# One 32-byte tile moved to the far end of SBUF, so that every tile starts at a multiple of 128 bytes

## The chip, the core and the metric

The kernel runs on one core of a Trainium2 chip. Its time is device microseconds of one execution. Five engines work side by side: TensorE (PE in the profile, its weight loads PEld), VectorE (DVE), ScalarE (ACT), GpSimd (POOL) and SyncE (SP), which issues the DMAs here. On-chip memory (SBUF) has 128 partitions; a tile of shape [128, n] has one row of n elements in each of them, and all rows of a tile begin at the same byte address.

## What is computed

All arrays are float32 (batch 8, heads 8, sequence 576, head size 64; 4608 tokens, model width 512):

```python
kv = einsum('bhsd,bhse->bhde', k, v)           # linear attention
out = einsum('bhsd,bhde->bhse', q, kv)
x = out / sqrt(mean(out * out, -1) + 1e-6) * g_norm
h = x @ w_in                                    # 512 -> 2048
x = (s * relu(h) ** 2 + b) @ w_out              # 2048 -> 512
h = maximum(maximum(x @ w1, x @ w2), x @ w3)    # 512 -> 768
return h @ w_out2                               # 768 -> 512
```

## The kernel before

TensorE multiplies in fp32r, a four-byte format of less precision, so each operand is split into a high and a low part (`hilo`: ScalarE copies the high part, VectorE subtracts) and each product is three matmuls: high by high, high by low, low by high. A matmul loads 128 columns of a weight tile (512 bytes of each row) and streams up to 512 columns of the other operand past it (2048 bytes of each row), which is called the moving operand below.

Tokens go in nine tiles of 512. In the first stage, per token tile and per chunk f of 16 chunks of the 2048 wide layer, `u1` (line 326) makes 12 matmuls `h<-xh,w` and `h<-xl,w`, `u1_end` squares and splits, and two chunks later `u2` (line 349) makes 12 matmuls `y<-gh,w` and `y<-gl,w`. Attention for the next tiles is put between them (`s1`, `s3`, `s4`: lines 215, 244, 284, 285; `ones` is the weight tile of lines 284 and 285). Until all weights are split (the first 300 us) `w_float` and `w_parts` turn them from 64 to 32 bits on ScalarE and VectorE. In the second stage `v1` (line 488) forms the products of the next layer by a seven-product scheme from prepared weight tiles `wc`, and `v2_steps` (line 557) the last product. The weights of the second stage are prepared in the last two token tiles of the first stage and pass through DRAM (`combine`, `pair_load`).

A scheduling layer sets each engine's order when the program is built. SBUF addresses come from pools that are stacked from the left end or, with `side="right"`, from the right end:

```python
const = pool("const", 1)                              # left, first
wpa = pool("wpa", 2 * FA, st=low, side="right")       # weights f < 8
wpb = pool("wpb", 2 * (KF - FA), st=mlp1)             # left: weights f >= 8
t = (wpa if f < FA else wpb).tile([P, 2, DM], F32R, tag="w", name=nm)   # FA = 8
cst = const.tile([P, 8], F32, name="cst")             # 32 bytes in a row
w2p["a"] = pool("w2a", 2, side="right")               # wc of q % 3 == 0, 1
w2p["b"] = pool("w2b", 1)                             # left: wc of q % 3 == 2
```

`ones` is the first tile, at byte 1152 (a multiple of 128). `cst` (scales, biases and two constants as single columns) follows it and takes 32 bytes, and every size after it is a multiple of 128, so that all later tiles of the left side begin 32 bytes past a multiple of 128. Those of the right side (`wpa`, `w2a` and the high parts of the tokens in the second stage, pool `ta`) begin 96 bytes past one. The moving operands of the first stage (`xh`, `xl`, `gh`, `gl`) lie left; those of the second stage lie right where they are high parts and left where they are low parts (with the first super-tile, which has 256 columns in place of 512, both lie right).

Of the kernel before, what the change touches and what calls it, by code (L numbers as in the profile page):

```python
# [8 lines left out]
F32 = mybir.dt.float32  # L9
# [11 lines left out]
P = 128  # L21
# [3 lines left out]
def fused_kernel(ctx, tc, qt, kv, kvr, g_norm, w_in, w_out, s, b, w1, w2, w3, w_out2, out):  # L25
# [22 lines left out]
    def pool(name, bufs, space=None, st=ctx, side="left"):  # L48
        kw = {"space": space} if space is not None else {"side": side, "reuse_waits": "tile"}
        return st.enter_context(tc.tile_pool(name=name, bufs=bufs, **kw))  # L50


    mlp1, attn, low = (ctx.enter_context(ExitStack()) for _ in range(3))
    const = pool("const", 1)
    dram = pool("dram", 1, DRAM)
    wpa = pool("wpa", 2 * FA, st=low, side="right")
    rawp = pool("rawp", 2, st=mlp1)
# [16 lines left out]
    EARLY = 2  # L74
    start = [wpb.tile([P, NP + 2, P], F32, tag="w", name=f"start{i}") for i in range(EARLY)]
    onesf, zero = start[0][:, NP, :], start[0][:, NP + 1, :]
    cst = const.tile([P, 8], F32, name="cst")
    g_sb, sb_sb, lnb, exb = cst[:, 0:1], cst[:, 1:3], cst[:, 3:4], cst[:, 4:5]
    kvbd = [const.tile([P, 2, P], F32R, name=f"kvbd{p}") for p in range(NP)]
    y_dr = [dram.tile([P, KD, TW], F32, name=f"y_dr{t}") for t in range(NTILE)]  # L80
# [742 lines left out]
```

## Time and profile before

| | us |
|---|---|
| median of 3 runs | 1486.7 (1486.1 to 1487.91) |
| the profiled execution's own time | 1486.8 |
| its span, first to last instruction | 1485.0 |
| PE busy | 1442.6 |
| VectorE busy | 901.0 |
| ScalarE busy | 618.8 |

The profiled execution agrees with the median to 0.1 us, so its span and the 1.8 us around it are the base of all sums. A busy PE says little by itself, since matmuls overlap in its records: one of 512 columns is recorded with some 390 ns while the next starts 230 ns after it. How quickly they follow each other is seen in the chain of work that ended last, which counts matmuls in a row and the time from the first to the end of the piece.

### The profile page before, as it was taken

The numbers are of one execution on the slowest core, as the hardware profiler recorded it, in microseconds if no ns is written. First come the engines' busy times: TensorE is split into PE (matmuls) and PEld (weight loads), VectorE is DVE, ScalarE is ACT, GpSimd is POOL, SyncE is SP. The second block draws the span as 40 slices with busy tenths as digits, with TensorE's granted clock in tenths as the row PEclk, the third lists the DMA queues.
The fourth block names the chain that finished last, engine by engine and source line by source line (L and its number), as shares of the span: only waits on it lengthen the run. The fifth ranks groups of instructions, "written<-read, shape, count | busy, mean of one in ns | idle before, by whom it ended". The sixth has DMA issues, their size and how long they took to land.

```text
span 1485.0 us, 18915 instructions
## 1 busy us (share of the span) xinstructions
PE 1442.6 (97%) x7010; PEld 1175.6 (79%) x7010; DVE 901.0 (61%) x1722; ACT 618.8 (42%) x1255; POOL 11.7 (1%) x41
## 2 busy tenths in 40 slices
PE   6799999999999999999999999989999999999998
PEld 4678877788888888888888888977888888888887
DVE  6899989874445454454545556647573672673561
ACT  5665457444455445455544443223231241232221
POOL 0000000000000000000000000000000000000000
PEclk9999999999999999999999999999999999999999
DMA  6556565731111112111013689976553553551521
GB/s 206 160 184 193 176 205 188 226 119 40 40 46 47 53 32 68 47 46 43 15 47 135 232 314 307 387 260 220 198 192 121 198 180 136 194 198 68 188 100 57
DMA packets 66556, 217.77 MB, mean 147 GB/s; under 512 B 7968, under 2 KB 19232, under 8 KB 60704
## 3 DMA queue, kind: packets, MB, share of 16 engines
q1 hardware_dynamic: 66464, 216.56, 42.7%
q8 instruction: 55, 0.90, 0.2%
q14 instruction: 37, 0.30, 0.1%
HBM read 165.41 MB, written 51.12 MB: 146 GB/s over the span
## 4 chain that ended last, share of the span: by engine, by line
PE 85%; DVE 6%; DMA 5%; ACT 3%; issue 1%; SPq 0%; ACTq 0%; DVEq 0%
PE y L349 23%; PE h L326 23%; PE r L488 14%; PE x L488 11%; PE o L557 10%; DMA raw<-in_w_out 1%; DMA raw<-in_w_in 1%; PE ops L244 1%; PE kvps L215 1%; DMA raw<-in_w 1%; DVE tb L108 1%; PE mps L282 1%; DMA wc<-wc_dr 1%; DMA out<-e 1%; ACT ta L105 0%
## 5 line engine op out<-in xcount | busy, mean ns | idle before, releaser
L326 PE MATMUL h<-xh,w 128*128 128x512 f32 (+1 forms) x1176 | 391.9, 394 | 3.4 <-ACT w L90 1.5
L349 PE MATMUL y<-gh,w 128*128 128x512 f32 (+1 forms) x1176 | 387.9, 391 | 2.3 <-ACT gh L337 2.2
L326 PEld LDWEIGHTS h<-xh,w 128*128 128x128 f32 x1176 | 221.5, 190 | 53.3 <-ACT xh L90 2.5
L349 PEld LDWEIGHTS y<-gh,w 128*128 128x128 f32 x1176 | 220.9, 189 | 51.1 <-ACT gh L337 3.6
L326 PE MATMUL h<-xl,w 128*128 128x512 f32 (+1 forms) x588 | 230.2, 392 | 0.1
L349 PE MATMUL y<-gl,w 128*128 128x512 f32 (+1 forms) x588 | 229.0, 390 | 0.0
L336 DVE SCALAR_TENSOR_TENSOR r<-r,cst 128x512 f32<-128x512 f32 (+1 forms) x147 | 108.7, 740 | 130.8 <-ACT r L335 130.1
L338 DVE SCALAR_TENSOR_TENSOR gl<-r,cst,gh 128x512 fp32r<-128x512 f32 (+1 forms) x147 | 108.8, 740 | 123.9 <-ACT gh L337 123.4
L496 ACT ACTIVATE s<-x 128x512 f32<-128x512 f32 (+1 forms) x135 | 74.8, 554 | 247.4 <-PE x L488 241.6
L337 ACT ACTIVATE gh<-r,cst 128x512 fp32r<-128x512 f32 (+1 forms) x147 | 104.9, 714 | 150.1 <-PE y L349 145.5
L335 ACT ACTIVATE r<-h 128x512 f32<-128x512 f32 (+1 forms) x147 | 86.5, 589 | 177.2 <-PE h L326 156.9
L501 DVE TENSOR_TENSOR c<-r,s 128x512 f32<-128x512 f32 (+1 forms) x135 | 81.9, 634 | 91.0 <-ACT s L496 90.6
L557 PE MATMUL o<-wo,hh 128*128 128x512 f32 x432 | 133.2, 390 | 0.3 <-ACT hh L90 0.3
L326 PEld LDWEIGHTS h<-xl,w 128*128 128x128 f32 x588 | 111.8, 190 | 23.5 <-DVE xl L91 0.5
L349 PEld LDWEIGHTS y<-gl,w 128*128 128x128 f32 x588 | 110.7, 188 | 21.7 <-DVE gl L338 0.2
L557 PEld LDWEIGHTS o<-wo,hh 128*128 128x128 f32 x432 | 80.7, 188 | 17.6 <-ACT hh L90 1.0
L557 PE MATMUL o<-wo,hl 128*128 128x512 f32 x216 | 83.8, 389 | 0.0
L501 DVE TENSOR_TENSOR u<-r,s 128x512 f32<-128x512 f32 (+1 forms) x45 | 28.7, 638 | 67.8 <-PE r L488 67.8
L105 ACT ACTIVATE ta<-raw 128x512 f32<-128x512 f32 x56 | 37.7, 674 | 44.6 <-DMA raw<-in_w_out 18.3
L488 PE MATMUL r<-b21h,wc 128*128 128x512 f32 x144 | 51.3, 395 | 4.6 <-ACT b21h L90 4.6
L488 PE MATMUL x<-t2h,wc 128*128 128x512 f32 x144 | 50.8, 393 | 1.1 <-ACT t2h L90 1.1
L488 PE MATMUL x<-t3h,wc 128*128 128x512 f32 x144 | 50.8, 393 | 0.8 <-ACT t3h L90 0.8
(140 smaller groups left out, 2066.8 us busy)
## 6 DMA issues: line engine op xcount, KB each, us to landing
wc<-wc_dr SPq DMA_DIRECT2D x45, 1792.0 KB, 7.4
kv<-in_kv SPq DMA_DIRECT2D x32, 512.0 KB, 4.3
y_dr<-st SPq DMA_DIRECT2D x56, 256.0 KB, 3.3
raw<-in_w_out SPq DMA_DIRECT2D x22, 512.0 KB, 3.7
raw<-in_w SPq DMA_DIRECT2D x18, 512.0 KB, 4.1
out<-e SPq DMA_DIRECT2D x36, 256.0 KB, 2.0
raw<-in_w_in SPq DMA_DIRECT2D x16, 512.0 KB, 3.9
y<-y_dr SPq DMA_DIRECT2D x32, 256.0 KB, 4.8
```

The source lines that it names most:

```text
L105: nc.scalar.activation(out=af, in_=high.bitcast(F32), func=ACTF.Abs)
L108: nc.vector.scalar_tensor_tensor(out=tb, in0=high, scalar=0xC0000000, in1=tb, op0=ALU.bitwise_and, op1=ALU.bitwise_or)
L326: nc.tensor.matmul(h[:, :n], lhsT=w[:, z, kk, :], rhs=x[:, kk, o:o + n], start=(i == 0), stop=(i == 3 * KD - 1))
L335: nc.scalar.activation(out=rn, in_=h[:, :n], func=ACTF.Relu)
L336: nc.vector.scalar_tensor_tensor(out=rn, in0=rn, scalar=sb_sb[:, 0:1], in1=rn, op0=ALU.mult, op1=ALU.mult)
L337: nc.scalar.activation(out=gh[:, :n], in_=rn, func=ACTF.Identity, bias=sb_sb[:, 1:2])
L338: nc.vector.scalar_tensor_tensor(out=gl[:, :n], in0=rn, scalar=sb_sb[:, 1:2], in1=gh[:, :n].bitcast(F32), op0=ALU.add, op1=ALU.subtract)
L349: nc.tensor.matmul(yt[t, o][j][:, :n], lhsT=w[:, z, c], rhs=r[:, :n], start=(f == fa and i == 0), stop=(f == fb - 1 and i == 2))
L488: nc.tensor.matmul(ps, lhsT=w[:, z, POS[c], kk * P:(kk + 1) * P], rhs=x, start=(first and i == 0), stop=(i == 3 * KD // 2 - 1), skip_group ...
L496: nc.scalar.activation(out=t, in_=ps, func=ACTF.Copy)
L501: nc.vector.tensor_tensor(out=o, in0=ps, in1=t, op=ALU.add)
L557: nc.tensor.matmul(acc[b], lhsT=l[:, o:o + P], rhs=wob[m][:, z, :], start=(m == 0 and i == 0), stop=(m == KM - 1 and i == 2))
```

## The change

`cst` leaves the left pool for one of its own, the first from the right end, and is declared with 96 bytes of a row in place of 32. The 32 bytes ahead of the left tiles are gone, and those of the right side move down by 96 bytes.

```diff
     const = pool("const", 1)
+    rim = pool("rim", 1, side="right")
...
-    cst = const.tile([P, 8], F32, name="cst")
+    cst = rim.tile([P, 24], F32, name="cst")
     g_sb, sb_sb, lnb, exb = cst[:, 0:1], cst[:, 1:3], cst[:, 3:4], cst[:, 4:5]
```

In the built programs the instructions of each engine, their order and their waits are the same. What differs is the SBUF address of every tile but `ones`. Counted over all SBUF tiles of the program, 1,975 that began 32 or 96 bytes past a multiple of 128 now begin at one. All of them are now an odd multiple of 128 bytes, not a multiple of 256. Addresses in PSUM and DRAM stay.

## Rows read from the trace of the kernel before

**Rows 1.** The page's part 1: busy time, share of the span, instructions.

```profile
PE 1442.6 (97%) x7010; PEld 1175.6 (79%) x7010; DVE 901.0 (61%) x1722; ACT 618.8 (42%) x1255; POOL 11.7 (1%) x41
```

**Rows 2.** Groups by line and shape: count, busy us, mean ns of one.

```profile
L326 PE MATMUL h<-xh,w 128*128 128x512 f32 x1128 | 379.3, 396 | 1.6 <-ACT xh L90 1.1 <-ACT r L335 0.4
L349 PE MATMUL y<-gh,w 128*128 128x512 f32 x1128 | 375.9, 394 | 0.0
L326 PE MATMUL h<-xl,w 128*128 128x512 f32 x564 | 222.6, 395 | 0.0
...
L557 PE MATMUL o<-wo,hh 128*128 128x512 f32 x432 | 133.2, 390 | 0.3 <-ACT hh L90 0.3
...
L488 PE MATMUL x<-b11h,wc 128*128 128x512 f32 x144 | 51.5, 398 | 0.0
...
L488 PE MATMUL x<-b11l,wc 128*128 128x512 f32 x72 | 28.7, 399 | 0.0
```

**Rows 3.** The chain, 483 to 545 us, one token tile: start us, us, what.

```profile
483.92 2.80 PE h L326 x12
...
489.80 0.44 PE ops L244 x3
490.24 2.80 PE h L326 x12
...
520.99 2.72 PE h L326 x12
...
527.39 2.73 PE h L326 x12
...
533.45 2.75 PE h L326 x12
536.21 0.12 PE mps L284
536.33 0.11 PE mps L285
```

**Rows 4.** The chain, 1118 to 1182 us, second stage.

```profile
1117.87 4.08 PE o L557 x18
...
1137.05 2.75 PE r L488 x12
...
1146.77 2.80 PE r L488 x12
...
1156.47 2.75 PE r L488 x12
...
1175.81 2.80 PE r L488 x12
```

**Rows 5.** The chain, 925 to 960 us, second stage with 256 columns.

```profile
930.93 0.72 PE r L488 x6
...
944.05 9.14 DMA wc<-wc_dr
...
954.25 0.68 PE x L488 x6
```

**Rows 6.** Stretches: length, busy us (count) of PE, PEld, DVE, ACT, POOL, PEclk, DMA.

```profile
0.00:74.00 74.00, 53.13 (x356) 39.17 (x357) 55.47 (x149) 45.44 (x111) 4.91 (x19) 0.95 0.57 183
74.00:297.00 223.00, 215.22 (x1036) 171.34 (x1035) 206.84 (x429) 124.14 (x248) 2.15 (x7) 0.98 0.63 195
297.00:860.00 563.00, 563.00 (x2795) 459.47 (x2794) 286.37 (x552) 270.60 (x577) 4.62 (x15) 1.00 0.22 71
860.00:960.00 100.00, 98.39 (x551) 86.20 (x550) 66.20 (x133) 38.75 (x75) 0.00 (x0) 1.00 0.90 326
960.00:1040.00 80.00, 71.60 (x358) 58.66 (x357) 45.83 (x86) 23.33 (x46) 0.00 (x0) 0.98 0.69 251
1040.00:1485.00 445.00, 441.29 (x1924) 360.74 (x1922) 240.29 (x376) 116.54 (x199) 0.00 (x0) 1.00 0.42 153
```

**Rows 7.** VectorE groups by shape: count, busy us, mean ns of one.

```profile
L501 DVE TENSOR_TENSOR c<-r,s 128x512 f32<-128x512 f32 x108 | 71.3, 687 | 73.2 <-ACT s L496 73.0
...
L501 DVE TENSOR_TENSOR c<-r,s 128x256 f32<-128x256 f32 x27 | 10.6, 421 | 17.8 <-ACT s L496 17.6
```

## The prediction

> **What bounds the kernel now.** I read the page's busy times first. PE is busy for 97% of the span, VectorE for 61% [rows 1]. The stretches say where that holds: from 297 to 860 us PE's busy time is the whole stretch, from 1040 us nearly, at a granted clock of 1.00, which is the level of 2.4 GHz, while VectorE and the DMA engines have room [rows 6]. There the time is the number of matmuls times the distance between their starts. Two stretches are not so. From 74 to 297 us VectorE is busy for 206.84 of 223 us, and from 860 to 1040 us the DMA engines are busy at a share of 0.90 and then 0.69 and PE stands idle for some 10 us [rows 6]; once PE waits 9.14 us for a weight tile `wc` [rows 5].
>
> So the view that decides is the chain, read for the distance from one matmul to the next. It has four different answers for matmuls of the same shape:
> - first stage, weights of the left pool (f from 8 on): 2.72 to 2.75 us for 12, so 226.7 to 229.2 ns each [rows 3]
> - first stage, weights of the right pool (f below 8): 2.80 us for 12, 233.3 ns [rows 3]
> - second stage: 2.75 us for 12 with `wc` at the right (two of three), 229.2 ns, and 2.80 with `wc` at the left (every third), 233.3 ns [rows 4]
> - the last product, all operands at the left: 4.08 us for 18, 226.7 ns [rows 4]
>
> A right operand begins 96 bytes past a multiple of 128, a left one 32. The pattern is: weights and moving operand with the same offset follow each other every 226.7 ns, with different offsets every 233.3 ns. The sides could differ for another reason than the offset, but `ones` lies at the left and has offset 0: with it as the next weights the distance is 0.12 us at 256 columns, with weights of offset 32 next it is 0.11 [rows 3]. The step of 10 ns in which the chain is printed makes this weak, but it points at the offset and not at the side.
>
> The second thing to see is what is left when the offsets agree. 256 columns with equal offsets take 0.72 us for 6, 120.0 ns [rows 5], and 512 take 226.7: 256 more columns cost 106.7 ns, one column per cycle of 2.4 GHz. By that rate 512 columns are 213.3 ns and 256 are 106.7, so both carry a surplus of 13.3 ns; 320 columns, at 0.44 us for 3 [rows 3], carry 146.7 - 133.3 = 13.3 too. And 13.3 ns are 32 columns, 128 bytes of a row. A row of 2048 bytes that starts inside a unit of 128 bytes touches 17 units, not 16; 17 times 13.3 ns is 226.7, and 9 and 11 units give the other two. That reading is an estimate of mine. A fixed price of 32 cycles per matmul would give the same three numbers. Against both in their strict form, 256 columns with unequal offsets take 0.68 us for 6, 113.3 ns [rows 5]: a surplus of half a unit, 64 bytes.
>
> **The change part by part.** No instruction is added, removed or moved.
>
> *Offsets become equal.* All weights and all moving operands now have offset 0. At the least this takes the 233.3 ns rows to 226.7. There are 3384 matmuls of 512 columns on lines 326 and 349 (1128 + 564 each; line 349's `gl` as many as `xl`), 1512 on line 488 (seven products of 144 + 72) and 648 on line 557 (432 and half as many) [rows 2]. The first take (233.3 + 227.9) / 2 = 230.6 ns in the mean, 227.9 being that of 2.72, 2.73 and 2.75 us for 12; the second (2 x 229.2 + 233.3) / 3 = 230.6; the third 226.7. To 226.7 this saves 4896 x 3.9 ns = 19 us.
>
> *Rows begin at a unit.* What the remaining 13.3 ns become is shown by no row, for no moving operand of before has offset 0. Bounds: all of it goes (213.3 ns, nothing below one column per cycle) or none (226.7). Between them lies 220.0, one half unit left, by the 113.3 ns row, where a half unit was left. I hold that the cut unit goes, and do not know whether a half unit stays, so I take the middle of 213.3 and 220.0, a surplus of 3.3 ns. That saves 4896 x 14.0 + 648 x 10.1 ns = 75.0 us, and on some 618 matmuls of 256 and 320 columns (378 of the first super-tile, 240 of attention) about 9 ns each, 5.6 us: 80.6 us. With none left it is 93.4 + 7.5 = 101 us; with a half unit left 56.2 + 3.4 = 60 us.
>
> The Trainium skill has a rule for the warm distance ("TensorE: Matmul & The Clock Gate", Back-to-back issue gap): N / 2.4 GHz plus 2.5 ns, 215.7 ns at 512 columns. By it the saving would be some 86 us before what is given back; no row here comes below 226 ns.
>
> *Given back.* Matmuls become 14 / 230 = 6.1% shorter. Of PE's 53 us before 74 us that is 3.2 us, and I count none: PE waits there for loads and VectorE. From 74 to 297 us it is 13.1 us; VectorE is at 93% and is not made shorter, so I keep a third and give back 8.7. From 860 to 1040 us it is 10.4 us of 170; the DMA engines are nearly full, so I give back half, 5.2. Together 17 us [rows 6].
>
> *VectorE, ScalarE, DMA.* If a cut unit cost VectorE too, it would be at most 64 bytes, 16 elements; an element costs (687 - 421) / 256 = 1.04 ns [rows 7], so 17 ns of an instruction, and for the 578 instructions before 297 us [rows 6] 10 us at most. Its 512-element time is one number in both pools, so I take nothing and keep the 10 us as a bound. Columns of `cst` are read as before, from another address. The transfers' bytes and rows stay; I take nothing for them, hidden by the matmuls except at 860 to 1040 us.
>
> Sum: 80.6 - 17.1 = 63.5 us; 1486.8 - 63.5 = 1423 us. With a half unit left 60 x 0.79 = 47 us and 1440; with none 101 x 0.79 = 80 us and 1407.
>
> **The rivals.**
>
> *Only the mismatch goes.* The 13.3 ns are a price of every fp32r matmul (a weight switch, say), not of a cut unit. For it: the same 13.3 at three widths. Against it: the 113.3 ns row, which undercuts it. 19 us less a fifth: 1472 us (1465 to 1479).
>
> *Nothing changes.* The sides differ by place and not by offset, and the rest is fixed. For it: side and offset go together for all operands but `ones`; against it: the `ones` rows. 1486.8 us. The Trainium skill speaks for this case ("SBUF — State Buffer", Specifications): it gives 16 bytes as the unit in which rows are read, and every offset of before is a multiple of that; in "TensorE: Matmul & The Clock Gate" (Step-by-step) the next weights are loaded through a port of their own and take nothing from the running matmul. The rows of 2.72 and 2.80 us disagree with the second.
>
> *Slower: aligned rows collide.* Both streams now begin a unit at the same byte, so if the two collide once more per matmul when they are in step, each pays a half unit more, 6.7 ns. For it: at 256 columns equal offsets cost 120.0 ns and unequal 113.3 [rows 5]. Against it: at 512 columns it is the other way round. All matmuls of 512 at 233.3 cost 4896 x 2.7 + 648 x 6.6 ns = 17.5 us, the smaller ones 4: 1508 us. It decides once the mean distance at 512 columns is above today's 230.1 ns.
>
> **How the numbers follow.** What a measurement of this kernel can tell from no change is about 0.2%, 3 us. Chances: the forecast, 1407 to 1440 us, 0.60, with 1423 as its time; still less than that (VectorE or the stretch before 297 us gains too) 0.05; only the mismatch 0.20; nothing 0.08; slower 0.07. The range from 1405 to 1475 us takes in the first and the third and leaves out 2 in 10. Faster 0.85, same 0.08, slower 0.07.
>
> **What would show it.** In the chain of the changed kernel one piece of 12 matmuls should take the same time in the first stage for all f and in the second for all q: 2.60 us (216.7 ns), 2.56 with no surplus, 2.64 with a half unit, 2.72 if only the mismatch goes, 2.72 and 2.80 as before if nothing does. VectorE's 687 ns should stay. From 74 to 297 us the same work should end some 4 us earlier, with VectorE's busy share at 95% or more; that would show what is given back. The forecast is wrong if the distance stays at 226 ns or above, or if it falls and the time is kept by waits for VectorE or `wc` that are not there now.

## The result, and the profile after

The changed kernel takes 1472.12 us (median of 4 runs, 1471.08 to 1474.7) beside 1487.31 of the kernel before: a ratio of 0.9898, with a 95% interval from 0.9879 to 0.9917. It is faster by 1.0%. The forecast of 1423 us was wrong, in size and not in direction; 1472 us is the time that the prediction gave to its rival "only the mismatch goes"; it lies at the far end of the whole range and outside the forecast's own, 1407 to 1440.

The page's busy times of the changed kernel, which answer to [rows 1]:

```profile
PE 1428.1 (97%) x7010; PEld 1175.7 (80%) x7010; DVE 900.1 (61%) x1722; ACT 619.1 (42%) x1255; POOL 11.7 (1%) x41
```

The chain of the changed kernel in the same token tile as [rows 3] (start us, us, what; line 326 is now 327, and so on):

```profile
479.03 2.72 PE h L327 x12
...
491.64 2.72 PE h L327 x12
...
515.68 2.72 PE h L327 x12
...
528.14 2.75 PE h L327 x12
530.88 0.12 PE mps L285
531.00 0.12 PE mps L286
...
539.94 2.72 PE h L327 x12
```

The chain in the second stage, three consecutive q, for [rows 4]:

```profile
1116.05 2.72 PE r L489 x12
...
1125.57 2.72 PE r L489 x12
...
1135.09 2.72 PE r L489 x12
```

In the second stage, where there were 2.75 and 2.80 us for 12 matmuls, there is now one number, 2.72, with right weights (the first piece) and left ones (the third), and for every q. In the first stage the 2.80 is gone, and 2.72 is what a piece takes that follows another piece of 12. A piece behind attention takes 2.74 to 2.75 us (2.95 behind `kvps`), as such pieces with left weights did before, so those 2 or 3 hundredths are no matter of offsets. So the difference between the sides is gone. But 2.72 is also the least that was there before: 226.7 ns for 512 columns, with the 13.3 ns over one column per cycle that the forecast took away. The two `mps` pieces of 256 columns were 0.12 and 0.11 us in [rows 3] and are 0.12 and 0.12 now, at equal offsets.

The chain near 940 us, for [rows 5]:

```profile
926.22 11.37 DMA wc<-wc_dr
...
938.67 0.72 PE x L489 x6
...
944.94 0.71 PE x L489 x6
```

With 256 columns equal offsets stay at 118 to 120 ns, as before; the 0.68 us of [rows 5] were those of unequal ones. The 9.14 us of `wc` in [rows 5] and the 11.37 us here are the time of a transfer that the chain follows back, and not a wait of PE, as the prediction read them. PE's own idle time before a `wc` was this in the kernel before (us in total, times, longest), and it is 0.2 us now:

```profile
PE r L488 <- DMA wc<-wc_dr: 1.5, 1, 1.5
```

The stretches, for [rows 6] (length, busy us and count of PE, PEld, DVE, ACT, POOL; granted clock; DMA share and GB/s):

```profile
0.00:74.00 74.00, 53.62 (x361) 39.71 (x362) 57.01 (x153) 46.72 (x114) 4.90 (x19) 0.96 0.58 185
74.00:297.00 223.00, 215.03 (x1043) 173.17 (x1043) 206.64 (x428) 123.63 (x245) 2.24 (x7) 0.98 0.63 198
297.00:860.00 563.00, 563.00 (x2828) 465.44 (x2827) 291.14 (x559) 275.01 (x583) 4.61 (x15) 1.00 0.23 76
860.00:960.00 100.00, 98.31 (x548) 85.37 (x547) 61.22 (x127) 35.09 (x71) 0.00 (x0) 1.00 0.91 329
960.00:1040.00 80.00, 72.56 (x362) 59.99 (x361) 48.85 (x88) 24.35 (x48) 0.00 (x0) 0.98 0.64 228
1040.00:1485.00 445.00, 425.59 (x1878) 352.05 (x1876) 235.28 (x369) 114.28 (x196) 0.00 (x0) 1.00 0.41 149
```

The counts show where the time came from. In the same 563 us PE starts 2828 matmuls and not 2795, 33 more; to 297 us it is 12 more (1404 and not 1392), and from 860 to 1040 us 1 more (910 and not 909). From 1040 us to the end of the span, 1469.3 us, PE has 1878 matmuls left in 429.3 us, where it had 1924 in 445.0: 228.6 ns each and not 231.3. The gain is made where PE has matmuls of 512 columns with unequal offsets one after another. From 860 to 1040 us there is none, and the DMA share of 0.91 need not be the reason: of some 900 matmuls that the kernel before starts there, only 69 are of 512 columns and have unequal offsets. VectorE is no quicker (for [rows 7]):

```profile
L502 DVE TENSOR_TENSOR c<-r,s 128x512 f32<-128x512 f32 x108 | 71.3, 688 | 70.5 <-ACT s L497 69.6
```

### The profile page after: what moved, and what is told of

Read it like the earlier page. It is cut to its first block, busy times and chain, and to the rows that moved or that the text cites. A ratio compares the mean times of both kernels' runs of the same rounds, so it can differ in the third digit from the quotient of the medians.

```text
span 1469.3 us, 18915 instructions
## 1 busy us (share of the span) xinstructions
PE 1428.1 (97%) x7010; PEld 1175.7 (80%) x7010; DVE 900.1 (61%) x1722; ACT 619.1 (42%) x1255; POOL 11.7 (1%) x41
## 4 chain that ended last, share of the span: by engine, by line
PE 83%; DVE 6%; DMA 6%; ACT 3%; issue 1%; SPq 0%; POOL 0%; ACTq 0%; DVEq 0%; POOLq 0%
PE y L350 22%; PE h L327 22%; PE r L489 14%; PE x L489 11%; PE o L558 10%; DMA raw<-in_w_in 2%; PE ops L245 1%; PE kvps L216 1%; DMA raw<-in_w 1%; DMA F<-wf_dr 1%; DVE tb L109 1%; DMA wc<-wc_dr 1%; DMA y<-y_dr 1%; DVE w L92 1%; PE mps L283 1%
## 5 line engine op out<-in xcount | busy, mean ns | idle before, releaser
L327 PE MATMUL h<-xh,w 128*128 128x512 f32 (+1 forms) x1176 | 387.0, 390 | 3.2 <-ACT w L91 1.5
```

The costliest lines, as they stand in the source:

```text
L327: nc.tensor.matmul(h[:, :n], lhsT=w[:, z, kk, :], rhs=x[:, kk, o:o + n], start=(i == 0), stop=(i == 3 * KD - 1))
```

## The experiments

**Is it the multiple of 128, or the difference?** Theory A: only the difference of the offsets of weights and moving operand counts. Theory B: a row has to begin at a multiple of 128. The first experiment (e1 below, the others by their first two letters likewise) adds one unused tile to the kernel before and aligns no tile to 128:

```diff
     const = pool("const", 1)
+    rim = pool("rim", 1, side="right")
+    rim.tile([P, 16], F32, name="pad")
```

> The kernel before with one unused tile of 64 bytes at the right end, so that right tiles begin 32 bytes past a multiple of 128, as the left ones do. No tile but ones is at a multiple of 128. Theory A (only the difference of the offsets of weights and moving operand counts): 2.72 us for 12 matmuls everywhere, as in the changed kernel, and 1472 us. Theory B (rows have to begin at a multiple of 128): right weights stay as dear as before, 2.80 us for 12, and 1487 us.

Measured: 1473.85 us, ratio 0.9913 (0.9896 to 0.9929). Its chain, with a piece of right and one of left weights:

```profile
478.92 2.73 PE h L328 x12
...
515.62 2.72 PE h L328 x12
```

The change's gain is there, within the intervals, with every row but those of `ones` 32 bytes past a multiple of 128. Theory B falls, and with it the reason that the change's name gives.

The next two leave the left tiles of the changed kernel and make a difference again:

```diff
-    cst = rim.tile([P, 24], F32, name="cst")
+    cst = rim.tile([P, 16], F32, name="cst")
```

> The changed kernel with 64 bytes at the right end in place of 96: left tiles at multiples of 128, right tiles 32 bytes past one. Theory A in the form that any difference costs the same 6.7 ns (as the rows with ones as weights let one think): 2.80 us for 12 with right weights in the first stage, 1487 us. Theory A in the form that only a difference of 64 bytes costs: 2.72 and 1472 us. Theory B: right rows are cut, 1487 us.

Measured: 1487.65 us, ratio 1.0009 (0.9998 to 1.0021), no different from the kernel before. The chain, right and then left weights:

```profile
479.14 2.80 PE h L327 x12
...
522.57 2.72 PE h L327 x12
```

A difference of 32 bytes costs what 64 did.

```diff
+    pad = pool("pad", 1, st=mlp1)
+    pad.tile([P, 16], F32, name="pad")
     wpb = pool("wpb", 2 * (KF - FA), st=mlp1)
...
-    cst = rim.tile([P, 24], F32, name="cst")
+    cst = rim.tile([P, 8], F32, name="cst")
```

> The mismatch doubled: weights of the first stage of both pools begin 64 bytes past a multiple of 128, the moving operands of the first stage at one; the second stage is as mixed as in the kernel before. Theory A: 2.80 us for 12 for all f, so against the changed kernel 3384 x 5.7 + 1512 x 3.8 ns = 25 us, of which four fifths show: 1492 us, slower than before by 5 us. If the side and not the offset were the cause: 2.80 for f below 8 alone and 1487 us.

Measured: 1494.18 us, ratio 1.0056 (1.0041 to 1.0071); 1492 was expected. The chain, f below 8 and from 8 on:

```profile
480.70 2.80 PE h L329 x12
...
518.70 2.80 PE h L329 x12
```

The left weights, which lie on the side of their moving operands, now cost 2.80 too. So the side is not the cause, the offset is.

One half of the change alone, on the kernel before: the left tiles 32 bytes lower, the right ones where they were. The size below is that of a reserved area at the left end.

```diff
-nc = _bacc.Bacc("TRN2", ..., dynamic_dma_scratch_size=1024)
+nc = _bacc.Bacc("TRN2", ..., dynamic_dma_scratch_size=992)
```

> One half of the change alone: the kernel before with all left tiles 32 bytes lower (at multiples of 128, ones and cst apart) and the right ones where they were, 96 bytes past one. Operands of the two sides then differ by 96 bytes. If any difference costs the same: 2.80 us for 12 with right weights, 1487 us, no gain from the aligned half. If each side gained by its own alignment: half of the change's gain, 1479 us.

Measured: 1489.17 us, ratio 1.0034 (1.0023 to 1.0046), so slightly slower than before. The chain, right and left weights, and a piece of the second stage:

```profile
479.84 2.80 PE h L326 x12
...
516.96 2.72 PE h L326 x12
...
1125.78 2.79 PE r L488 x12
```

Aligning one side alone is worth nothing. It is even a little dearer than the old difference: in the second stage all pieces of 12 take 2.79 us in this kernel, where [rows 4] have two of three at 2.75.

**Modulo what?** The next two kernels start from the changed one. The first puts all tiles at multiples of 256, the second moves the left ones alone, by the second of these edits:

```diff
-    cst = rim.tile([P, 24], F32, name="cst")
+    cst = rim.tile([P, 56], F32, name="cst")
...
-nc = _bacc.Bacc("TRN2", ..., dynamic_dma_scratch_size=1024)
+nc = _bacc.Bacc("TRN2", ..., dynamic_dma_scratch_size=896)
```

> The changed kernel with every tile moved to a multiple of 256 bytes (128 bytes less ahead of the left tiles, 128 more at the right end); in the changed kernel all tiles are at odd multiples of 128. Theory C (the remaining 13.3 ns are a cut unit of 256 bytes): 2.56 us for 12 matmuls and some 1400 us. Theory D (they are a price of the matmul that no offset changes): 2.72 us for 12 and 1472 us.

Measured: 1471.99 us, ratio 0.9911 (0.9892 to 0.993), and 2.72 us for 12:

```profile
478.49 2.72 PE h L327 x12
...
515.14 2.72 PE h L327 x12
```

Theory C falls: no unit of 256 bytes is cut. The 13.3 ns have now stayed at three common offsets modulo 256: 0 here, 128 in the changed kernel and 160 in e1.

> The changed kernel with the left tiles at multiples of 256 and the right ones at odd multiples of 128, so that operands of the two sides differ by an odd multiple of 128 bytes, and no longer by a multiple of 256. If the offsets count modulo 128: 2.72 us for 12 and 1472 us. If they count modulo 256: 2.80 with right weights and 1487 us.

Measured: 1485.9 us, ratio 1.0005 (0.9994 to 1.0016), the gain is gone. The chain, two right pieces and a left one:

```profile
476.40 2.77 PE h L327 x12
...
485.96 2.80 PE y L350 x12
...
511.14 2.72 PE y L350 x12
```

So multiples of 128 are not even enough: both sides of this kernel have them, and it is as slow as before. With right weights and left moving operands the differences that were free are 0 (e1) and 256 bytes (the changed kernel and e4), those that cost are 32 (e2), 64 (before, e3), 96 (g2) and 128 (f4). In the trace of the changed kernel, with the addresses of the built program beside it, the differences between weights and moving operand are 0, 256, 512 and 768 modulo 1024, and the mean distance at 512 columns is 227 ns at each of them. The change works because 96 bytes at the right and none at the left happen to put the two sides a multiple of 256 apart.

**What are the 13.3 ns that stay?** Half of the weight columns are loaded by two of three matmuls of `u1` (which leaves out half of those parts), once at equal offsets and once on the kernel of e3:

```diff
-            for z, x in ((0, xh), (0, xl), (1, xh)):
-                nc.tensor.matmul(h[:, :n], lhsT=w[:, z, kk, :], ...)
+            parts = ((0, xh, P), (0, xl, P // 2), (1, xh, P // 2))
+            for z, x, m in parts if kk < KD - 1 else parts[::-1]:
+                nc.tensor.matmul(h[:m, :n], lhsT=w[:, z, kk, :m], ...)
```

> The changed kernel, where two of the three matmuls of each triple on the line of u1 load 64 weight columns in place of 128 (half of the output rows miss these parts); they stream 512 columns as before. If the 13.3 ns that stay at equal offsets go with the bytes of the weight load, the two halves bring 12 matmuls from 2.72 to about 2.67 us; if they are a price of each matmul, 2.72 stays.

Measured: 2.75 us for 12, a little more and not less. The little more comes from the changes of length: by the start times in the trace, the 279 matmuls of 64 weight columns that stand between two of 64 are followed by the next after 227.4 ns, as those of line 327 in the changed kernel are, and where 64 and 128 meet it is about 230 ns.

```profile
480.04 2.75 PE h L328 x12
...
492.73 2.75 PE h L328 x12
```

> The same half loads on e3_weights64, where weights and moving operands of the first stage differ by 64 bytes. If the 6.7 ns of a difference are paid for each weight load whatever its length, 12 matmuls take what f1_half_load takes and 0.08 us more; if they go with the bytes of the load, 0.05 us more or less than that.

Measured: 2.79 us, 0.04 more than f1, between the two answers. The start times say more: between two loads of 64 columns the distance is 232.3 ns, beside 227.4 in f1, and with whole loads it is 233.3 (e3) beside 227.4. So 4.9 of 5.9 ns are still paid with half the bytes.

```profile
484.71 2.79 PE h L330 x12
...
497.55 2.79 PE h L330 x12
```

The 13.3 ns do not go with the bytes of the load, and the price of a difference at most in small part. Then the first stage in a two-byte type:

```diff
-    t = (wpa if f < FA else wpb).tile([P, 2, DM], F32R, tag="w", name=nm)
+    t = (wpa if f < FA else wpb).tile([P, 2, DM], BF16, tag="w", name=nm)
...   # the same for xh, xl, gh, gl
```

> The changed kernel with the parts of weights, x and g of the first stage in bfloat16 (the result is less exact), so that a matmul reads 1024 bytes of the moving row and 256 of the weights in place of 2048 and 512. If the 13.3 ns belong to four-byte rows, the distance at 512 columns comes to 213 to 216 ns, 2.56 to 2.59 us for 12; if they are a fixed price of a matmul with a new weight load, 2.72 stays.

Measured: 2.59 us for 12, 215.8 ns; one run of 1441.55 us.

```profile
479.19 2.59 PE h L328 x12
...
525.11 2.59 PE h L328 x12
```

> f3_bf16 (first stage in bfloat16) with its weights 64 bytes off its moving operands, as in e3_weights64. If a difference costs by itself, the distance at 512 columns rises from 216 to about 222 ns and 12 matmuls take 2.66 us; if it costs only where four-byte rows are read at full rate, 2.59 stays.

Measured: 2.59 us again, with a difference of 64 bytes between weights and moving operands (its time, 1448.41 us in one run, is not comparable, since its second stage is mixed again).

```profile
479.24 2.59 PE h L330 x12
481.83 2.59 PE y L353 x12
```

So both prices, the 13.3 ns that stay and the 6.7 ns of a difference, are paid with fp32r operands and not with bfloat16 ones: there 2.5 ns are left of the first, and nothing of the second at the one difference that was tried. Whether the width of the rows decides or the number format is not separated by these runs.

## Why the prediction was wrong

**The step that failed** is "I hold that the cut unit goes". The prediction took the 13.3 ns for a cut unit of 128 bytes and left the fixed price, which gave the same three times, to a rival. No row had a moving operand at offset 0 to choose between them. The runs put the price in the unit's place: 2.72 us for 12, 226.7 ns each, at every common offset that was tried, so the distance stayed above the 226 ns that the prediction had named as its sign of being wrong. Of the 80.6 us only the part from equal offsets stood, which the rival had alone.

**The row that misled** was the 0.68 us for 6 matmuls of 256 columns [rows 5], taken as proof that a surplus can be under 13.3 ns, and so as a sign against the rival. It came from unequal offsets, which shorten the distance at 256 columns and lengthen it at 512. Why they do the first is open.

**Equal offsets become cheaper: right, and sized a little large.** 2.80 and 2.75 fell to 2.72 us. That the offset and not the side counts was right too (e1 and e3), and that 32 bytes are enough for the price (e2). The term was 19 us. Compared matmul by matmul in the two traces (from one start to the next, where both are under 300 ns, so that no long wait lies between), those of 512 columns gain 15.7 us: 10.0 in the first stage and not 13.2, in part because the 2.75 us behind attention, which the mean of 227.9 ns took in, stays; and 5.6 in the second stage. Nor does one price hold for every difference: in [rows 4] with `wc` at the left, 8 of 12 matmuls have unequal offsets and 4 equal ones, which at 233.3 and 226.7 ns gives 2.77 us, and the row has 2.80. And the `ones` rows from which the offset was inferred did not bear it: with all offsets equal both of their pieces take 0.12 us, so the 0.11 was no sign of equal offsets. It was called weak, and was weaker than that.

**Given back: the size was luck.** A fifth of 19 us was to be lost, leaving 15, and the profiled executions differ by 1486.8 - 1471.1 = 15.7 us. But the same comparison of the traces shows no loss to waits: the time in which starts are 300 ns or more apart becomes shorter by some 1 us. What PE gains on 512 columns is 2.8 us before 297 us, 7.2 to 860, 0.4 to 1040 and 5.3 after that. The matmuls of 256 columns, which were to gain, lose 1.3 us, since their unequal offsets were the cheaper ones. So the rival's 1472 us, too, was met with one term too large and a loss that did not come.

**VectorE and transfers at nothing: right.** VectorE's sum takes 687 and 688 ns, and PE's idle time before a `wc` did not grow (1.5 us before, 0.2 now).

**The collision and "nothing changes": wrong here.** Aligned rows cost no more than rows that share another offset. The Trainium skill's rule on the weight path ("TensorE: Matmul & The Clock Gate", Step-by-step), that a load of the next weights takes no read bandwidth from the running matmul, agrees with g1 in bfloat16. In e2, e3 and f4 the distance changes where only addresses do, which that rule does not provide for; that it is the load which takes something from the stream is not shown. The Trainium skill's warm distance for an isolated matmul, N / 2.4 GHz plus 2.5 ns (the same page, Back-to-back issue gap), by that sum an estimate of 215.8 ns at 512 columns, is met by f3 at 215.8 and missed by all fp32r rows of 512 columns here, at 226.7 or more.

**What stays open.** What happens in the chip when weights and moving operand in fp32r start at different offsets, and what the 13.3 ns are, is not shown. These runs say that the 13.3 ns are there in fp32r and nearly gone in bfloat16, and that they do not depend on the load's bytes. Differences below 32 bytes were not tried.

## What to carry to other kernels

Where fp32r matmuls of 512 columns follow each other without a wait, keep all their SBUF operands, weights and moving, at one offset modulo 256 bytes; of the three offsets tried here, which one was of no account. At 256 columns this gains nothing: there unequal offsets were the quicker ones (113.3 beside 120.0 ns). The change cost 64 bytes of SBUF here and was worth 1%. Look at where the two ends of SBUF put the tiles: a small tile at either end shifts one side against the other, and the chain's time for a dozen matmuls shows it at once (2.72 against 2.80 us). When two readings of a surplus give the same numbers at every width on the page, keep both in the forecast, and do not let one exception choose between them. And when the sum comes out, look whether its terms did.

## What was not expected of the hardware

At a granted clock of 1.00 the same matmul of 512 fp32r columns takes 226.7 or 233.3 ns depending only on the address of its weights against that of its moving operand, and a difference of 128 bytes costs about as much as one of 32. In bfloat16 it is 215.8 ns whether the offsets agree or differ by 64 bytes. So a matmul of 512 columns takes 5% longer in fp32r than in bfloat16 in this kernel, and 8% with the dearer offsets.
